# LSH attention with two GLU layers: the hash as four raw fp32 products of 32 columns, codes in rounded fp32

## The chip, the core and the metric

The program runs on one core of a Trainium2 chip. The metric is the device time of one execution in microseconds (us). TensorE (PE) multiplies and transposes, VectorE (DVE), ScalarE (ACT) and GpSimd (POOL) work elementwise, and the SP queue (and ACT's own queue at the start) issues the transfers.

## What is computed

Attention comes first, for 2 batches of 8 heads with 768 tokens and 64 numbers per head. A query sees only the keys whose hash bucket is the same as its own; a bucket is made of the signs of six projections.

```python
q_bits = (np.einsum('bhsd,dk->bhsk', q, proj) > 0).astype(np.int64)
k_bits = (np.einsum('bhsd,dk->bhsk', k, proj) > 0).astype(np.int64)
powers = 2 ** np.arange(n_bits)
q_bucket = np.sum(q_bits * powers, axis=-1)
k_bucket = np.sum(k_bits * powers, axis=-1)
mask = q_bucket[:, :, :, None] == k_bucket[:, :, None, :]
scores = scale * np.matmul(q, k.transpose(0, 1, 3, 2))
scores = np.where(mask, scores, -1000000000.0)
...
return np.matmul(attn, v).astype(np.float32)
```

The softmax of the masked scores is multiplied with v. Two gated layers (512 to 1536 to 512, and 512 to 2048 to 512) follow on all 1536 tokens. The change touches only the hash.

## The kernel before

Attention works on 8 pairs of heads, one after the other. The two heads of a pair share a tile: 64 partitions each (`E` and `O`), 768 tokens along the free dimension. For each pair a `Prep` object makes ready what the next pair needs while the pair before it is in the main loop:

- `UW`, or `scale`, `top` and `rest`: the loaded tile `nat` (named `n` in the profile) is split into `U`, its value rounded to fp32r, and `W`, what is left. For the first pair ACT and DVE do this, for the others POOL.
- `z`: the projections. The table `pz` holds the projection matrix (again as a rounded part and a rest). Twelve products of 384 columns add into one PSUM tile: for queries and keys, `U` with the first part of `pz`, `U` with the rest, and `W` with the first part, each for two halves of the tokens. The table is shifted in its columns so that each of the four cases lands on its own rows of the 72 that a product writes.
- `bits`: ACT takes the sign and writes `bt` in bf16.
- `xp`: four products (`code` times `bt`, 384 columns each, bf16) count for each of the 64 buckets how many bits agree. `Hot` turns that into a one-hot row, big for queries and minus one for keys, which is added to the scores as extra rows of the contraction. DMAs (`copy`, `first_moves`, `swap`) and copies put the pieces of `U`, `W` and the one-hot rows on their partitions.

The scores of a unit (`QK`, 128 queries of one head) are four products of 384 columns; DVE takes the maximum, ACT the exponential (`P`). `Flip` transposes P on TensorE into `pt`, and ACT and DVE write it as two fp16 parts. `pv` multiplies with v in 64 columns of the array per head, so its products come in pairs, one for each half of the columns.

The order on each engine is written out by hand: every step has a time in a table (`AT` for the first and the last pair, `AM` for the six between them, in units of a score tile), and the program is emitted in order of these times. Nothing is reordered by a scheduler. The four parts of `z` stand there as `"Z"`, the sign as `"BITS"`, the code products as `"XP"`.

The first pair's preparation is written out by itself at the start. `warm` runs products of the zeroed tile `bt` while the first loads are under way. In that stretch ACT makes `U`, then copies `H` (line 430) and `B` (line 434) for queries, takes the sign (line 401), copies the second `B`, and writes the one-hot rows `N` and `H` (line 412). The first scores (`sc`, line 474) need `N`.

Of the kernel before, what the change touches and what calls it, by code (L numbers as in the profile page):

```python
# [29 lines left out]
def lsh_attention_glu_act(ctx, tc, qt, kt, v, proj, w_gate, w_val, w_out1, w_in2, w_out2, ident_d, code_d, out):  # L30
    nc = tc.nc
# [22 lines left out]
    proj_sb = const.tile([128, NB], F32, name="proj_sb")  # L54
    ZR = 32 + 4 * NB
    ZW = 72
    Z0 = 32 + 2 * NB
    code_f = const.tile([ZR, 2, 2, 128], F32, name="code_f")
# [3 lines left out]
    pz = const.tile([128, 2, Z0 + ZW], F32R, name="pz")  # L62

    def constants():
        nc.scalar.dma_start(proj_sb, proj)
        nc.scalar.dma_start(code_f, code_d)
        nc.scalar.dma_start(ident, ident_d)
        nc.vector.memset(bt, 0.0)
        nc.vector.memset(pz.bitcast(F32), 0.0)
        nc.gpsimd.memset(code, 0.0)  # L70
        for i, c in enumerate((-TINY, -2.0 * BIG, -float(NB), 0.5, -1.0)):
            nc.vector.memset(cst[:, i:i + 1], c)
        for e, r in ((0, E), (1, O)):
            cs = slice(Z0 + e * NB, Z0 + (e + 1) * NB)
            nc.vector.tensor_copy(pz[r, 0, cs], proj_sb[r])
            nc.vector.tensor_tensor(out=pz[r, 1, cs], in0=proj_sb[r], in1=pz[r, 0, cs].bitcast(F32), op=ALU.subtract)
# [252 lines left out]
    def qbank(k, g):  # L329
# [6 lines left out]
        if next(turn) < 4:  # L336
            nc.tensor.matmul(t, lhsT=code[:, 0, 0, :], rhs=bt, start=True, stop=True, skip_group_check=True)
        return t

    with ExitStack() as actx:  # L340
# [18 lines left out]
        class Prep:  # L359
# [225 lines left out]
        with tc.manual_schedule():  # L585
# [39 lines left out]
            def scale_in():  # L625

                nc.tensor.matmul(idle[:, 2, 0:1], lhsT=code_f[0:1, 0, 0, :], rhs=VS[seq[0]][0][:, 132:133], start=True, stop=True)
# [779 lines left out]
```

## Time and profile before

| what | us |
|---|---|
| median of 3 runs (lowest, highest) | 783.62 (782.73, 785.25) |
| the profiled execution | 782.68 |
| span of the profiled execution, first to last instruction | 780.9 |
| PE busy | 767.5 (98%) |
| DVE busy | 624.8 (80%) |
| ACT busy | 523.5 (67%) |
| POOL busy | 165.3 (21%) |

Attention takes the first 236 us or so, the two gated layers the rest. A share of busy time is a mean over both. The end of a matmul is modelled in the trace: a row's duration holds the time in the pipeline too, so what a product costs in a stream is read from the start of one row to the start of the next.

### The profile page before, as it was taken

To read this page: it belongs to the slowest core of one execution; us is meant where nothing else is said; L and a number is where in the kernel's file an instruction comes from. 1 tells how busy PE (TensorE), PEld (TensorE's weight loads), DVE (VectorE), ACT (ScalarE), POOL (GpSimd) and SP (SyncE) were. 2 spreads that over 40 slices of the span, in tenths; PEclk is the share of its full clock that TensorE was granted. 3 is DMA by queue.
4 is the path that set the end of the run, shared out by engine and by line. 5 is a ranking of instruction groups with operands and counts; after the bars stand their busy time and mean duration, and the time that the engine had idled before them with its cause. 6 is when DMAs were issued, how large, how long until landed. Compare 5 with 4: busy or idle time off the path is not lost.

```text
span 780.9 us, 13062 instructions
## 1 busy us (share of the span) xinstructions
PE 767.5 (98%) x4912; PEld 701.8 (90%) x4912; DVE 624.8 (80%) x1095; ACT 523.5 (67%) x1027; POOL 165.3 (21%) x166
## 2 busy tenths in 40 slices
PE   8999999999999999999999999999999999999997
PEld 5778888888778999999999999998999998898986
DVE  6879999988978978877869869868989867666643
ACT  6988899988975566566555544446666667676653
POOL 5746677864594000000000000000000000000000
PEclk9999999999999999999999999999999999999999
DMA  8845466435101122131122422433332201000002
GB/s 241 201 118 152 92 176 173 130 85 123 32 1 55 55 97 67 55 101 62 55 81 81 136 81 91 126 109 108 108 95 95 81 1 74 8 1 1 0 1 82
DMA packets 41462, 66.98 MB, mean 86 GB/s; under 512 B 5630, under 2 KB 28542, under 8 KB 41398
## 3 DMA queue, kind: packets, MB, share of 16 engines
q1 hardware_dynamic: 40608, 65.30, 28.7%
q8 instruction: 39, 0.64, 0.3%
q10 hardware_dynamic: 790, 0.84, 0.3%
q14 instruction: 25, 0.20, 0.1%
HBM read 45.27 MB, written 3.15 MB: 62 GB/s over the span
## 4 chain that ended last, share of the span: by engine, by line
PE 66%; DVE 1%; ACT 0%; issue 0%; ACTq 0%
PE qa L297 3%; PE qa L296 3%; PE qa L298 3%; PE p L298 3%; PE p L296 3%; PE p L297 3%; PE qb L296 2%; PE y L297 2%; PE y L298 2%; PE y L296 2%; PE qe L296 2%; PE qe L297 2%; PE qe L298 2%; PE qb L297 2%; PE qb L298 2%; PE qa L1167 2%
## 5 line engine op out<-in xcount | busy, mean ns | idle before, releaser
L521 DVE SCALAR_TENSOR_TENSOR PT<-pt,PT 128x512 f16<-128x512 f32 x144 | 95.2, 685 | 13.4 <-ACT PT L518 10.5
L482 DVE TENSOR_REDUCE st<-sc 128x1 f32<-128x768 f32 x96 | 90.5, 948 | 6.6 <-PE sc L474 6.4
L518 ACT ACTIVATE PT<-pt 128x512 f16<-128x512 f32 x144 | 80.6, 596 | 20.9 <-PE pt L509 19.4
L486 ACT ACTIVATE P<-sc,st 128x768 f32<-128x768 f32 x96 | 86.9, 905 | 8.2 <-DVE st L482 8.0
L509 PE MATMUL pt<-ident,P 128*128 128x128 f32 x576 | 78.5, 276 | 2.4 <-DVE PT L521 1.3
L509 PEld LDWEIGHTS pt<-ident,P 128*128 128x128 f32 x576 | 65.0, 141 | 12.9 <-DVE PT L521 7.3
L566 PE MATMUL O<-PT,vh 128*64 128x256 f16 x576 | 53.8, 277 | 0.0
L298 PE MATMUL p<-yh,whl_i 128*128 128x384 f32 x128 | 42.9, 336 | 0.0
L296 PE MATMUL p<-yh,whl_i 128*128 128x384 f32 x128 | 42.9, 335 | 0.0
L297 PE MATMUL p<-yl,whl_i 128*128 128x384 f32 x128 | 42.9, 335 | 0.0
L566 PEld LDWEIGHTS <-vh 128*64 128x64 f16 x576 | 31.3, 109 | 10.5 <-issue 9.8
L1144 ACT ACTIVATE t<-p,cst 128x384 f32<-128x384 f32 x32 | 18.3, 573 | 27.1 <-PE p L298 27.1
L566 PE MATMUL O<-PT,vl 128*64 128x256 f16 x288 | 33.8, 273 | 0.0
L474 PE MATMUL sc<-H,H 128*128 128x384 f32 x96 | 28.3, 376 | 1.1 <-ACT P L486 1.0
L1149 DVE SCALAR_TENSOR_TENSOR gg<-p,t 128x384 f32<-128x384 f32 x32 | 17.7, 554 | 13.3 <-ACT t L1146 13.2
L474 PE MATMUL sc<-N,N 128*128 128x384 f32 x96 | 28.0, 372 | 0.4 <-ACT N L412 0.3
L261 ACT ACTIVATE qb<-qa 128x384 f32<-128x384 f32 x24 | 11.4, 475 | 24.0 <-PE qa L298 13.5
L261 ACT ACTIVATE qd<-qb 128x384 f32<-128x384 f32 x24 | 11.4, 475 | 23.8 <-PE qb L298 20.4
L389 POOL TENSOR_TENSOR W<-n,U 128x768 fp32r<-128x768 f32 x14 | 25.6, 1830 | 0.2
L474 PE MATMUL sc<-U,U 128*128 128x384 f32 x96 | 24.7, 338 | 0.0
L296 PEld LDWEIGHTS p<-yh,whl_i 128*128 128x128 f32 x128 | 24.0, 188 | 0.5
L297 PEld LDWEIGHTS p<-yl,whl_i 128*128 128x128 f32 x128 | 24.0, 188 | 0.5
(1220 smaller groups left out, 2535.2 us busy)
## 6 DMA issues: line engine op xcount, KB each, us to landing
wr_o<-in_moe_w_out_dram SPq DMA_DIRECT2D x28, 512.0 KB, 3.3
H<-U SPq DMA_DIRECT2D x29, 192.0 KB, 3.7
wr_i<-in_moe_w_in_dram SPq DMA_DIRECT2D x8, 512.0 KB, 3.7
wr_i<-in_moe_w_in_dram SPq DMA_DIRECT2D x16, 256.0 KB, 2.8
n<-in_qt_dram SPq DMA_DIRECT2D x8, 384.0 KB, 6.7
n<-in_kt_dram SPq DMA_DIRECT2D x8, 384.0 KB, 6.0
U<-W SPq DMA_DIRECT2D x16, 192.0 KB, 4.9
vr<-in_v_dram SPq DMA_DIRECT2D x8, 384.0 KB, 5.4
```

The lines of the kernel that those rows point to most:

```text
L261: nc.scalar.activation(out=self.new("bcd"[m]), in_=src, func=AF.Copy)
L296: nc.tensor.matmul(ps, lhsT=wh, rhs=rh, start=first, stop=False, **kw)
L297: nc.tensor.matmul(ps, lhsT=wh, rhs=rl, start=False, stop=False, **kw)
L298: nc.tensor.matmul(ps, lhsT=wl, rhs=rh, start=False, stop=last, **kw)
L389: nc.gpsimd.tensor_tensor(out=self.t4[j][1], in0=self.nat[j], in1=f(self.t4[j][0]), op=ALU.subtract)
L474: nc.tensor.matmul(self.sc[:, n, 0:HN], lhsT=M[:, ts], rhs=K[:, n * HN:(n + 1) * HN], start=s0, stop=not s0)
L482: nc.vector.tensor_reduce(out=self.st[:, 0, self.c:self.c + 1], in_=self.sc[:, :, 0:HN], op=ALU.max, axis=AX.XY, negate=True)
L486: nc.scalar.activation(out=self.P, in_=self.sc[:, :, 0:HN], func=AF.Exp, bias=self.st[:, 0, self.c:self.c + 1], scale=1.0, accum_out=self. ...
L509: nc.tensor.transpose(self.ps[m][:, j, :], un[2 * self.n + e].P[:, a, c:c + 128], ident)
L518: nc.scalar.activation(out=self.part(0, m), in_=self.ps[m], func=AF.Copy, scale=PSCALE)
L521: nc.vector.scalar_tensor_tensor(out=self.part(1, m), in0=self.ps[m], scalar=PSCALE, in1=self.part(0, m), op0=ALU.mult, op1=ALU.subtract)
L566: nc.tensor.matmul(O_ps[r, 0:GN], lhsT=vv[m][:, e, i * D:(i + 1) * D], rhs=PT[:, l, e * NI + i, :], start=(s == 0), stop=(s == len(steps) ...
```

## The change

The projections become four products of the raw loaded tile with the raw projection matrix, both in plain fp32, one for each of queries and keys and token half. Each writes 32 rows of its own in PSUM, that is, uses 32 columns of the array. All four are issued at one place of the program, where the last part of `z` stood; the three earlier places in the tables are gone. `bt` and `code` become fp32r, on all 128 partitions: each of the four cases has its 32 partitions, and a code product contracts over these 32 rows instead of 128. The tables are loaded straight into place (`pz` by two transfers behind a memset), so the casts on DVE go; `code` is smaller. At the start the sign of the first pair stands ahead of the copies on ACT, `swap` ahead of the copies too, and `warm` has 16 products of fp32r instead of 18 of bf16.

```diff
-    code = const.tile([128, 2, 2, 128], BF16, name="code")
-    bt = const.tile([128, HN], BF16, name="bt")
+    ZC = 32
+    pz = const.tile([128, ZC], F32, name="pz")
+    ones = const.tile([1, 128], F32, name="ones")
+    code_f = const.tile([128, 128], F32, name="code_f")
+    code = const.tile([128, 128], F32R, name="code")
+    bt = const.tile([128, HN], F32R, name="bt")
...
-        nc.scalar.dma_start(proj_sb, proj)
+        nc.gpsimd.memset(pz, 0.0)
+        for e, r in ((0, E), (1, O)):
+            nc.scalar.dma_start(pz[r, e * NB:(e + 1) * NB], proj[r])
...
-            def z(self, lo, hi):
-                if lo == 0:
-                    self.z_ps = pA.tile([128, 512], F32, tag="mm", bufs=MMB, name=f"z_{self.b}_{self.p}")
-                steps = [(j, c, t, n) for j in range(2) for c, t in ((0, 0), (1, 0), (0, 1)) for n in range(2)]
-                for m in range(lo, hi):
-                    j, c, t, n = steps[m]
-                    s = Z0 - 32 * n - 2 * NB * j
-                    nc.tensor.matmul(self.z_ps[0:ZW, 0:HN], lhsT=pz[:, c, s:s + ZW], rhs=self.t4[j][t][:, n * HN:(n + 1) * HN], start=(m == 0), stop=(m == len(steps) - 1))
+            def z(self):
+
+                self.z_ps = pA.tile([128, 512], F32, tag="mm", bufs=MMB, name=f"z_{self.b}_{self.p}")
+                for g in range(4):
+                    j, n = divmod(g, 2)
+                    nc.tensor.matmul(self.z_ps[ZC * g:ZC * g + ZC, 0:HN], lhsT=pz, rhs=self.nat[j][:, n * HN:(n + 1) * HN], start=True, stop=True, skip_group_check=True)
 
             def bits(self):
-                nc.scalar.activation(out=bt[0:ZR], in_=self.z_ps[0:ZR, 0:HN], func=AF.Sign, bias=cst[0:ZR, 0:1])
+                nc.scalar.activation(out=bt, in_=self.z_ps[:, 0:HN], func=AF.Sign, bias=cst[:, 0:1])
+
+            def codes(self, ps, j, n):
+
+                r = slice(ZC * (2 * j + n), ZC * (2 * j + n) + ZC)
+                nc.tensor.matmul(ps, lhsT=code[r], rhs=bt[r], start=True, stop=True)
...
-            warm(18)
+            warm(16)
             pp, p1 = Prep(*seq[0]), Prep(*seq[1])
+            nc.vector.tensor_copy(code, code_f)
             pp.UW(0)
             pp.first_moves(0)
             pp.UW(1)
             pp.first_moves(1)
-            nc.vector.tensor_copy(code[0:ZR], code_f)
+            pp.z()
+            pp.bits()
             pp.first_copy(nc.gpsimd.tensor_copy, 0)
...
-            pp.first_copy(nc.scalar.copy, 1)
-            pp.rest_copy(0)
-            pp.z(0, 12)
             for j in range(2):
                 pp.swap(j)
-            pp.bits()
+            pp.rest_copy(0)
             pp.rest_copy(1)
+            pp.first_copy(nc.scalar.copy, 1)
...
-                "Z": (-1.4412, 0.5823, 0.8230, 1.7397),
+                "Z": (1.7397,),
```

On PE the place where the second pair of heads runs and the third is made ready shows what moves. Before, its twelve products stand in four groups of three, of which the last three groups are among these rows (`sc` are scores, `pt` transposes of P, `r` transposes of the row sums, `z` the projections):

```order
L398 MATMUL z_2_532<-U_0_2_446,pz 72x384
L398 MATMUL z_2_532<-W_0_2_447,pz 72x384 x2
L509 MATMUL pt_2_617<-ident,P_0_1_5_462 128x128 x4
L509 MATMUL pt_0_626<-ident,P_1_0_0_555 128x128 x4
L398 MATMUL z_2_532<-U_0_2_450,pz 72x384 x3
L474 MATMUL sc_1_1_1_642<-N_0_1_137,N_0_1_133 128x384 x2
L474 MATMUL sc_1_1_1_642<-W_0_1_135,W_0_1_131 128x384 x2
L398 MATMUL z_2_532<-U_0_2_450,pz 72x384
L398 MATMUL z_2_532<-W_0_2_451,pz 72x384 x2
L743 MATMUL r_0_1_5_657<-ident,rb_0_1_5_655 128x128 x2
```

Only the four new products are left, in two rows between the scores and the transposes of the row sums, where the last group was:

```order
L507 MATMUL pt_2_588<-ident,P_0_1_5_440 128x128 x4
L507 MATMUL pt_0_597<-ident,P_1_0_0_529 128x128 x4
L472 MATMUL sc_1_1_1_610<-N_0_1_132,N_0_1_128 128x384 x2
L472 MATMUL sc_1_1_1_610<-W_0_1_130,W_0_1_126 128x384 x2
L391 MATMUL z_2_615<-n_0_2_217,pz 32x384 x2
L391 MATMUL z_2_615<-n_0_2_219,pz 32x384 x2
L740 MATMUL r_0_1_5_627<-ident,rb_0_1_5_625 128x128 x2
```

The first group of three (ahead of the rows shown) is gone as well, and everything else on PE keeps its order. In this place ACT's order does not change.

At the start ACT's order does change. Before, it makes `U` for queries and keys, two copies, the sign `bt`, one more copy, and then the one-hot rows from `xq`:

```order
L379 ACTIVATE U_0_0_126<-n_0_0_78 128x768
L430 CAST H_0_0_124<-U_0_0_122 64x768
L434 CAST B_140<-W_0_0_123 64x768
L401 ACTIVATE bt<-z_0_158,cst 56x384
L434 CAST B_144<-W_0_0_127 64x768
L412 ACTIVATE N_0_0_125<-xq,cst 64x768
L412 ACTIVATE H_0_0_124<-xq,cst 64x768
```

Now the sign comes right behind `U`, and all three copies stand between it and the one-hot rows:

```order
L374 ACTIVATE U_0_0_121<-n_0_0_78 128x768
L394 ACTIVATE bt<-z_0_144,cst 128x384
L432 CAST B_136<-W_0_0_118 64x768
L432 CAST B_140<-W_0_0_122 64x768
L428 CAST H_0_0_119<-U_0_0_117 64x768
L410 ACTIVATE N_0_0_120<-xq,cst 64x768
L410 ACTIVATE H_0_0_119<-xq,cst 64x768
```

Two copies have moved from ahead of the sign to behind it. On DVE the cast of `code` moves ahead of the two `W`, and the four small instructions that made `pz` are gone.

## Rows read from the trace of the kernel before

**Rows 1.** The page: busy time and share, and TensorE's granted clock in 40 slices.

```profile
PE 767.5 (98%) x4912; PEld 701.8 (90%) x4912; DVE 624.8 (80%) x1095; ACT 523.5 (67%) x1027; POOL 165.3 (21%) x166
PEclk9999999999999999999999999999999999999999
```

**Rows 2.** Windows: stretch, then busy us and instructions by engine, clock, DMA.

```profile
0.00:12.00 12.00, 9.90 (x44) 5.74 (x45) 6.66 (x21) 7.53 (x9) 6.72 (x9) 1.00 0.77 232
12.00:40.00 28.00, 26.22 (x195) 21.37 (x194) 23.93 (x37) 22.63 (x49) 17.05 (x18) 1.00 0.85 213
96.00:124.00 28.00, 28.00 (x256) 24.49 (x254) 26.02 (x43) 25.18 (x53) 22.08 (x24) 1.00 0.64 173
```

**Rows 3.** Waits from 12 to 236 us: us in total, times, longest.

```profile
PE pt L509 <- DVE PT L521: 1.3, 3, 0.9
...
PEld L566 <- issue: 9.3, 44, 0.3
...
PEld L407 <- issue: 3.5, 18, 0.2
```

**Rows 4.** Instructions of line 398: duration ns (min/median/max), first and last start.

```profile
L398 PE MATMUL z<-U,pz x64: 331/337/469, 5.7 to 183.1; 128*72 128x384 f32 x64
L398 PE MATMUL z<-W,pz x32: 331/338/398, 6.8 to 183.4; 128*72 128x384 f32 x32
```

**Rows 5.** Timeline of PE around the last group of z: start, us, instruction.

```profile
100.82 0.51 PE L474 MATMUL sc<-W,W 128*128 128x384 f32 x2
101.17 0.34 PE L398 MATMUL z<-U,pz 128*72 128x384 f32 x1
101.34 0.51 PE L398 MATMUL z<-W,pz 128*72 128x384 f32 x2
101.69 0.38 PE L743 MATMUL r<-ident,rb 128*128 128x128 f32 x2
```

**Rows 6.** Instructions of line 627, the one raw fp32 product: duration, starts.

```profile
L627 PEld LDWEIGHTS idle<-vrow,code_f x2: 181/182/184, 19.2 to 19.3; 1*128 1x128 f32 x2
L627 PE MATMUL idle<-vrow,code_f x2: 245/256/266, 19.2 to 19.3; 1*128 1x1 f32 x2
```

**Rows 7.** Timeline of PE from 106.02 us.

```profile
106.02 1.04 PE L509 MATMUL pt<-ident,P 128*128 128x128 f32 x8
106.81 0.60 PE L474 MATMUL sc<-N,N 128*128 128x384 f32 x2
...
109.82 0.28 PE L566 MATMUL O<-PT,vl 128*64 128x256 f16 x2
110.03 0.34 PE L407 MATMUL xp<-bt,code 128*128 128x384 bf16 x1
110.30 0.30 PE L566 MATMUL O<-PT,vh 128*64 128x256 f16 x2
110.43 0.28 PE L566 MATMUL O<-PT,vl 128*64 128x256 f16 x2
110.54 0.28 PE L566 MATMUL O<-PT,vh 128*64 128x256 f16 x2
```

**Rows 8.** Timeline of the first 11 us, all engines.

```profile
1.11 4.92 PE L619 MATMUL idle<-bt 128*128 128x384 bf16 x18 [1.11 <-DVE bt L68]
...
5.49 0.85 ACT L379 ACTIVATE U<-n 128x768 fp32r<-128x768 f32 x1 [0.54 <-DMA n<-in_kt_dram]
5.74 0.99 PE L398 MATMUL z<-U,pz 128*72 128x384 f32 x4
...
8.42 0.58 ACT L401 ACTIVATE bt<-z,cst 56x384 bf16<-56x384 f32 x1 [0.50 <-PE z L398]
...
8.90 0.82 ACT L434 CAST B<-W 64x768 fp32r<-64x768 f32 x1
...
9.62 0.90 ACT L412 ACTIVATE N<-xq,cst 64x768 fp32r<-64x768 f32 x1
...
10.62 0.63 PE L474 MATMUL sc<-N,N 128*128 128x384 f32 x2 [0.27 <-ACT N L412]
```

More of the change, by code (lines that the diff above doesn't have):

```diff
@@ L53, in lsh_attention_glu_act @@
     ident = const.tile([128, 128], F32, name="ident")
[L54 to L58, printed above, removed]
-    code = const.tile([128, 2, 2, 128], BF16, name="code")
-    bt = const.tile([128, HN], BF16, name="bt")
+    ZC = 32
[4 more added lines that the diff above has]
+    bt = const.tile([128, HN], F32R, name="bt")
     cst = const.tile([128, 5], F32, name="cst")
-    pz = const.tile([128, 2, Z0 + ZW], F32R, name="pz")
     def constants():
-        nc.scalar.dma_start(proj_sb, proj)
+        nc.gpsimd.memset(pz, 0.0)
+        for e, r in ((0, E), (1, O)):
+            nc.scalar.dma_start(pz[r, e * NB:(e + 1) * NB], proj[r])
         nc.scalar.dma_start(code_f, code_d)
         nc.scalar.dma_start(ident, ident_d)
-        nc.vector.memset(bt, 0.0)
-        nc.vector.memset(pz.bitcast(F32), 0.0)
-        nc.gpsimd.memset(code, 0.0)
+        nc.vector.memset(bt.bitcast(F32), 0.0)
+        nc.vector.memset(ones, 1.0)
         for i, c in enumerate((-TINY, -2.0 * BIG, -float(NB), 0.5, -1.0)):
             nc.vector.memset(cst[:, i:i + 1], c)
[L73 to L76, printed above, removed]
     def f(ap):
@@ L336, in qbank @@
         if next(turn) < 4:
-            nc.tensor.matmul(t, lhsT=code[:, 0, 0, :], rhs=bt, start=True, stop=True, skip_group_check=True)
+            nc.tensor.matmul(t, lhsT=code, rhs=bt, start=True, stop=True, skip_group_check=True)
         return t
@@ L406, in xp @@
                     if n is None or n == a:
-                        nc.tensor.matmul(self.x_ps[:, a] if n is None else self.x_ps, lhsT=code[:, a, j, :], rhs=bt, start=True, stop=True)
+                        self.codes(self.x_ps[:, a] if n is None else self.x_ps, j, a)
             def Hot(self, j, dst, r, n=None):
@@ L625, in scale_in @@
             def scale_in():
-                nc.tensor.matmul(idle[:, 2, 0:1], lhsT=code_f[0:1, 0, 0, :], rhs=VS[seq[0]][0][:, 132:133], start=True, stop=True)
+                nc.tensor.matmul(idle[:, 2, 0:1], lhsT=ones, rhs=VS[seq[0]][0][:, 132:133], start=True, stop=True)
             def scale_keep():
@@ L645, in lsh_attention_glu_act @@
                 p1.rest(j)
-            nc.gpsimd.memset(code_f[0:1, 0, 0], 1.0)
-            pp.first_copy(nc.scalar.copy, 1)
-            pp.rest_copy(0)
-            pp.z(0, 12)
             for j in range(2):
                 pp.swap(j)
-            pp.bits()
+            pp.rest_copy(0)
             pp.rest_copy(1)
+            pp.first_copy(nc.scalar.copy, 1)
             xq = sc_tile("xq")
@@ L657, in lsh_attention_glu_act @@
                 for a in range(2):
-                    nc.tensor.matmul(xk[a] if j else xq[:, a, 0:HN], lhsT=code[:, a, j, :], rhs=bt, start=True, stop=True)
+                    pp.codes(xk[a] if j else xq[:, a, 0:HN], j, a)
             for dst, r in ((3, E), (2, O)):
@@ L825, in lsh_attention_glu_act @@
                         for m in range(1, 3):
-                            at(T["Z"][3] + 0.01 * m + 0.001 * j, 0, q, on, q + 1, "copy", j, m)
+                            at(T["Z"][0] + 0.01 * m + 0.001 * j, 0, q, on, q + 1, "copy", j, m)
                         at(T["H"][2 * j + 1] + 0.03, 0, q, on, q + 1, "copy", j, 3)
                         at(T["H"][3] + 0.035 + 0.005 * j, 0, q, on, q + 1, "copy", j, 4)
-                        at(T["TOP"][j] + 0.002 if q else T["Z"][3] + 0.03, 0, q, on, q + 1, "copy", j, 5)
-                    at(max(T["H"][3], T["Z"][3]) + 0.06, 0, q, on, q + 1, "done")
+                        at(T["TOP"][j] + 0.002 if q else T["Z"][0] + 0.03, 0, q, on, q + 1, "copy", j, 5)
+                    at(max(T["H"][3], T["Z"][0]) + 0.06, 0, q, on, q + 1, "done")
                 if q + 2 < NQ:
@@ L1374, in _tables @@
     sgn = (2 * bit - 1).astype(np.float32)
-    code = np.zeros((32 + 4 * nb, 2, 2, 2 * nbk), np.float32)
+    code = np.zeros((128, 2 * nbk), np.float32)
     for n in range(2):
@@ L1378, in _tables @@
             for e in range(2):
-                r = 32 * n + nb * (2 * j + (e ^ j))
-                code[r:r + nb, n, j, (1 - e) * nbk:(2 - e) * nbk] = sgn.T
+                r = 32 * (2 * j + n) + nb * (e ^ j)
+                code[r:r + nb, (1 - e) * nbk:(2 - e) * nbk] = sgn.T
     return {"ident": np.eye(128, dtype=np.float32), "code": code}
```

2 lines of the change are left out of this document (1 added, 1 removed), and 2 rows, old and new, of the table AT.

## The prediction, on record before the run

> **What bounds the kernel now.** The page comes first: PE is busy for 98% of the span, and its clock stands at its upper level, 2.4 GHz, in all 40 slices [rows 1]. That share is a mean, so the stages come next, as windows. From 96 to 124 us, which is attention in full swing, PE is busy 28.00 of 28 us, while DVE has about 2 us to spare and ACT nearly 3 [rows 2]. From 12 to 40 us, the first pair of heads, PE lacks 1.8 us and from 0 to 12 us 2.1 us [rows 2]: there a chain of single steps sets the pace. The waits agree: over the whole of attention PE's longest wait in total is 1.3 us, for DVE's second halves of P [rows 3], which is next to nothing. So a microsecond more or less of PE's stream between 40 and 236 us is a microsecond of the result, and at the start the chain through ACT has to be followed. The two layers behind 236 us are untouched.
>
> **What is removed from PE.** The projections are 64 + 32 products [rows 4], twelve for each of eight pairs. A row's duration (0.33 us) holds the pipeline, so the price is read between starts: one product from 101.17 to 101.34 us, two more to 101.69 [rows 5], 0.17 us each. That is 384 columns at one column per cycle. Twelve are 2.04 us per pair, and they fit between scores and transposes without a gap (scores at 100.82, two products, then 101.17).
>
> **What a raw fp32 product costs.** The trace has one, and of a single column: it stands as two weight loads and two matmuls [rows 6], so one instruction is two passes. How long 384 columns take in a pass it doesn't show. The nearest rows are the transposes of P, raw fp32 too: eight of 128 columns go by from 106.02 to 106.81 us [rows 7], 0.10 us each, or 0.11 by their own length (1.04 less the last one's 0.27, over seven). That is nearly two cycles a column; three of them make 384 columns, 0.30 to 0.33 us. I take 0.32 us for a pass, 0.64 for a product. The lower bound is the fp32r rate, 0.17 for a pass. The Trainium skill (FP8 and Floating Point Precision, TensorE Precision Notes) says that true fp32 makes four passes through the array; by it a product would be 4 x 0.16 = 0.64 us, an estimate, and the sum the same.
>
> **Whether the four overlap.** Each writes its own 32 columns of the array. The trace has products side by side in half the columns each: the pairs with v start at 110.43 and 110.54 us [rows 7], 0.11 us for two products of 256 columns, the time of one. So different columns do work at once. But PE starts matmuls in order, and the second pass of a product needs the columns of its first. With passes 1a 1b 2a 2b 3a 3b 4a 4b, 1b waits for 1a; 2a starts with 1b, 2b waits for 2a, and 3a starts with 2b. This makes five steps, 5 x 0.32 = 1.6 us per pair. If nothing overlaps it is 8 x 0.32 = 2.56 us, if all four run at once 2 x 0.32 = 0.64. I take the staircase: it needs only what the pairs show.
>
> **What is added by changing the cut of the array.** Between PV's pairs and a product over all columns there is a loss. The last pair starts at 109.82 us and should take 0.11, but the code product starts at 110.03: 0.10 lost. It takes 0.16, but the next pair starts at 110.30: 0.11 lost [rows 7]. The weight loads show it as a wait called "issue", 44 times before PV and 18 times before the code product, 0.2 us each [rows 3]: the load isn't made ahead as elsewhere. The Trainium skill (TensorEngine Tiling (Array Packing), Key Properties) says that a change of tiling mode drains TensorE; it speaks against this change, and the trace agrees with 0.1 us each way. I put 0.11 us on each new change. The block of projections in 32 columns has two (scores before, transposes behind). The code products contract over 32 rows now, a cut that the trace doesn't show; bounds are nothing and 0.11 us, and I take 0.11, as PV's columns are the only cut seen. In the six middle pairs three of the four code products gain one change each (the order has them between PV and something over the whole array; the fourth stands in PV on both sides and pays already). Together five changes, 0.55 us. In the first pair the four stand between transposes and scores: eight, with the block ten, 1.1 us.
>
> The code products themselves stay at 0.17 us: 384 columns, fp32r as fast as bf16 [rows 5, 7]. The sign's time hangs on 384 numbers per partition, which stay. Casts and memsets that go from DVE and POOL lie in the first microseconds, beside the loads.
>
> **The sum in the stream.** Six middle pairs: 1.6 - 2.04 + 0.55 = +0.11 us each, together +0.7. The pair prepared in the first pair's loop: 1.6 - 2.04 + 1.1 = +0.66; PE has some idle there, I count half, +0.3.
>
> One long block in place of four short ones could starve DVE and ACT. Ahead of the block stand two transposes' groups and a unit of scores: DVE has two halves of P and a maximum to do, ACT two more and an exponential, some 2 us, as long as the block. The sign isn't later than before either, since the groups left out earlier bring everything forward. I count nothing; without that cover it is what the block exceeds 2 us by, which is the serial rival.
>
> **The start.** Before, warm-up products run from 1.11 us to the first projection at 5.74; the sign runs from 8.42, half a microsecond after ACT was free, since it waited for the last of them, one copy follows at 8.90, and the one-hot `N` at 9.62, which releases the first scores at 10.62 [rows 8]. Now two late warm-up products are fewer (0.16 each), but a bigger memset of `bt` comes first, so the projections begin at about 5.55; the keys are there at 5.49 [rows 8]. They end 1.6 us later, with 0.17 for the pipeline at 7.3, and the sign begins at 7.35. ACT gives 0.48 us to the sign (8.42 to 8.90) and 0.72 to a copy (8.90 to 9.62) [rows 8]; three copies stand ahead of `N` now, so `N` begins at 7.35 + 0.48 + 3 x 0.72 = 10.0 in place of 9.62: the saved time is eaten by two copies that had been done while ACT waited for z. +0.4 us. What is late next is the first maximum and exponential; nothing else is awaited there, so I count it in full.
>
> **The sum**: +0.7 + 0.3 + 0.4 = +1.4 us. The profiled execution took 782.68 us (780.9 of span and 1.8 around it), which becomes 784.1; the median of the runs lies 0.9 above it, so I say **785.0 us**. A measurement of this kernel can tell about 0.3% from no change, 2.4 us: this is no change.
>
> **The rivals.**
> - *Nothing overlaps*: the second pass's weight load in the same columns holds up what is behind it, and passes run one by one. For it: two loads to a product [rows 6], and that no raw product in a part of the columns is in the trace; against it: the pairs with v. Middle pairs 2.56 - 2.04 + 0.55 = +1.07 each, +6.4; first loop half of +1.62; the start 0.96 later, +1.36: **+8.6 us, 792**. It decides from about 1.9 us a block on.
> - *All four at once*: 0.64 us a block. Middle pairs -0.85 each, -5.1; first loop -0.15; the start -0.5: **-5.8 us, 778**. Against it is the second pass behind the first in order. The Trainium skill (TensorE: Matmul & The Clock Gate, Part 3) says so: products in different columns start about 4 ns apart, and a pack lasts as long as one.
> - *A pass at the fp32r rate*, 0.17 us: the staircase is 0.85 us, middle pairs -0.64 each, -3.8; first loop nothing; the start -0.35: **-4.1 us, 779.5**. The transposes speak against it, unless weight loads and not columns set their pace.
> - *The code products pay nothing* for 32 rows: -0.33 x 6 and -0.4, so **-1 us, 782.6**, still no change.
>
> **Chances.** The staircase 0.52 (with or without the code products' price: same 0.37, slower 0.10, faster 0.05), nothing overlaps 0.30 (slower), all at once 0.10 and the fast pass 0.04 (faster), and 0.04 for something at the start that makes it slower (a late table, a clock that falls in the longer gap before the first scores). Faster 0.19, same 0.37, slower 0.44. The range leaves out the parallel case and the far end of the serial one: **779.5 to 793**; the likeliest case alone is 782.5 to 787.5.
>
> **What would show it.** In the profile after: projections as 8 matmuls a pair; the time from the first one's start to the transposes behind it, 1.8 us by the staircase, 2.8 serial, 0.9 parallel, and whether the starts of passes come 0.32 us apart in twos; "issue" waits of the weight loads at every code product; `N` at about 10.0 us at the start; the end of attention 1 to 2 us later. I am wrong if PE turns out to wait for ACT or DVE behind the block, or if a pass isn't 0.32 us.

## The result, and the profile after

The changed kernel takes 789.16 us (median of 6 runs, 787.24 to 790.68) against 783.17 us before (median of 6): a ratio of 1.0072, 95% interval 1.0059 to 1.0084. It is slower by 6 us. The profiled execution took 789.67 us with a span of 787.9 us, 7.0 us more than before's span.

The page of the changed kernel, busy time and PE's granted clock, to set beside [rows 1]:

```profile
PE 770.1 (98%) x4878; PEld 697.0 (88%) x4878; DVE 622.8 (79%) x1091; ACT 524.2 (67%) x1027; POOL 164.0 (21%) x165
PEclk8999999999999999999999999999999999999999
```

PE has 34 matmuls fewer, is busy 2.6 us longer, and no longer holds its clock in the first slice. Where the 7 us arise is read from the starts of the sign (one ACT instruction for each pair): the time from one to the next is the period of a pair. In us:

| kernel | first sign | to the 2nd | first loop | 2nd to 6th loop | last sign | span |
|---|---|---|---|---|---|---|
| before | 8.4 | 13.1 | 25.3 | 27.1, 28.0, 27.3, 27.3, 27.3 | 183.8 | 780.9 |
| after | 7.7 | 16.5 | 27.2 | 27.1, 28.0, 28.0, 28.0, 28.0 | 190.3 | 787.9 |

So the second sign is 2.6 us late, the first loop adds 1.85 us, the last three of these loops (the steady pairs) 0.7 us each, and 0.5 us arises behind the last sign. The first three parts have their rows below.

**The steady pair.** PE's timeline of the changed kernel around one block of projections (start, us, instruction), beside [rows 5]:

```profile
155.44 1.09 PE L507 MATMUL pt<-ident,P 128*128 128x128 f32 x8
...
157.46 1.26 PE L507 MATMUL pt<-ident,P 128*128 128x128 f32 x8
...
159.52 1.26 PE L507 MATMUL pt<-ident,P 128*128 128x128 f32 x8
...
161.40 0.85 PE L391 MATMUL z<-n,pz 128*32 128x384 f32 x8
162.19 0.44 PE L740 MATMUL r<-ident,rb 128*128 128x128 f32 x2
```

The block is eight matmuls, and the next instruction starts 0.79 us behind its first. Its own instructions, in a view that groups them by start (first line up to 161.45 us):

```profile
L391 PE MATMUL z<-n,pz x4: 510/510/510, 161.4 to 161.4; 128*32 128x384 f32 x4
...
L391 PE MATMUL z<-n,pz x8: 486/498/510, 161.4 to 161.8; 128*32 128x384 f32 x8
```

Four start together at 161.4 us, the other four up to 161.8. The experiment with one column group below shows that passes in the same columns run one behind the other, so these are all four first passes at once, then all four second passes.

Between the transposes `pt` the reader is to see their distance: 2.02 and 2.06 us. The same place of the kernel before, with three projections in each of these gaps:

```profile
149.34 1.03 PE L509 MATMUL pt<-ident,P 128*128 128x128 f32 x8
...
151.43 1.17 PE L509 MATMUL pt<-ident,P 128*128 128x128 f32 x8
...
153.67 1.04 PE L509 MATMUL pt<-ident,P 128*128 128x128 f32 x8
```

There it was 2.09 and 2.24 us. Taking 0.5 us of products out of a gap has brought 0.07 to 0.18 us. DVE's rows of the changed kernel show why:

```profile
156.71 1.29 DVE L519 SCALAR_TENSOR_TENSOR PT<-pt,PT 128x512 f16<-128x512 f32 x2
157.92 0.95 DVE L480 TENSOR_REDUCE st<-sc 128x1 f32<-128x768 f32 x1
158.78 1.29 DVE L519 SCALAR_TENSOR_TENSOR PT<-pt,PT 128x512 f16<-128x512 f32 x2
```

Two halves of P and one maximum follow each other without a pause, every 2.07 us. From 154.4 to 162.4 us DVE is busy 7.91 of 8 us (ACT 7.45); in the 20 us ahead of that, which hold the pair's four code products, only 16.9 of 20. The waits from 12 to 236 us (PE, then its weight loads) say what holds the transposes now, beside [rows 3]:

```profile
PE pt L507 <- DVE PT L519: 2.6, 2, 2.3
...
PEld pt L507 <- DVE PT L519: 10.3, 30, 2.6
PEld L564 <- issue: 8.7, 42, 0.3
...
PEld xp L399 <- issue: 3.6, 19, 0.2
```

The view of before that [rows 3] is taken from has this line for the loads as well:

```profile
PEld pt L509 <- DVE PT L521: 7.3, 23, 1.3
```

A transpose's buffer is free only when DVE has written the second half of P out of it; the transposes' loads wait 10.3 us for that, before 7.3. In the windows of [rows 2] PE had nothing to spare. It still seems so (27.88 of 28.00 us busy from 134.4 to 162.4 us), because such a wait sits inside a group of eight: the row grows from 1.03 to 1.26 us and counts as busy.

**The start.** All engines of the changed kernel, beside [rows 8]:

```profile
1.30 5.49 PE L617 MATMUL idle<-bt 128*128 128x384 f32 x16 [1.30 <-DVE bt L68]
...
6.72 0.85 PE L391 MATMUL z<-n,pz 128*32 128x384 f32 x8
7.66 0.58 ACT L394 ACTIVATE bt<-z,cst 128x384 fp32r<-128x384 f32 x1 [1.46 <-PE z L391]
...
8.18 0.82 DVE L634 CAST code<-code_f 128x128 fp32r<-128x128 f32 x1 [6.75 <-DMA code_f<-in_code_dram]
8.92 1.81 DVE L375 SCALAR_TENSOR_TENSOR W<-n,U 128x768 fp32r<-128x768 f32 x2
...
9.90 1.70 ACT L432 CAST B<-W 64x768 fp32r<-64x768 f32 x2 [1.66 <-DVE W L375]
...
12.24 0.89 ACT L410 ACTIVATE N<-xq,cst 64x768 fp32r<-64x768 f32 x1
...
13.23 0.98 PE L472 MATMUL sc<-N,N 128*128 128x384 f32 x2 [2.83 <-ACT N L410]
```

The sign comes 0.8 us earlier than before. But `code` is cast ahead of the two `W` on DVE now, and its table lands at 8.2 us; `W` starts at 8.92 where it started at 5.33, the copies `B` wait for `W`, and the one-hot `N` stands behind them. The first scores start at 13.23 in place of 10.62 us. PE has little to do from 10 to 13 us, and its clock falls. Windows, in the columns of [rows 2]:

```profile
10.00:11.00 1.00, 0.41 (x2) 0.00 (x0) 1.00 (x2) 0.96 (x2) 0.93 (x2) 0.54 0.42 117
12.00:13.00 1.00, 0.00 (x0) 0.00 (x0) 0.73 (x2) 1.00 (x2) 1.00 (x1) 0.50 0.88 194
15.00:16.00 1.00, 1.00 (x5) 1.00 (x4) 0.85 (x1) 0.12 (x1) 0.97 (x1) 0.50 1.06 375
```

A granted clock of 0.50 is the lower level, 1.2 GHz: there two score products take 0.64 us where they take 0.35 at 2.4 GHz.

**The first loop.** The SP queue, DVE and PE of the changed kernel:

```profile
37.10 2.70 SPq L450 DMA_DIRECT2D H<-U  x4
39.84 0.83 SPq L529 DMA_DIRECT2D vrow<-vm  x1
...
44.76 0.28 DVE L538 TENSOR_REDUCE vrow<-vrow 1x1 f32<-1x129 f32 x1 [2.78 <-DMA vrow<-vm]
...
46.90 1.65 PE L507 MATMUL pt<-ident,P 128*128 128x128 f32 x8 [2.25 <-DVE PT L519]
```

DVE stands 2.78 us in a step that belongs to v (the maximum of the next pair's v, which a small transfer brings to one partition), and PE waits 2.25 us for DVE. Before, these were 2.02 and 0.92 us:

```profile
41.45 0.27 DVE L540 TENSOR_REDUCE vrow<-vrow 1x1 f32<-1x129 f32 x1 [2.02 <-DMA vrow<-vm]
...
43.60 1.26 PE L509 MATMUL pt<-ident,P 128*128 128x128 f32 x8 [0.92 <-DVE PT L521]
```

Here too the clock follows:

```profile
44.00:46.00 2.00, 0.65 (x4) 0.33 (x2) 1.18 (x4) 0.00 (x0) 0.00 (x0) 1.00 0.00 0
46.00:48.00 2.00, 1.10 (x7) 0.92 (x8) 2.00 (x5) 1.40 (x3) 0.34 (x1) 0.90 0.32 43
48.00:50.00 2.00, 2.00 (x11) 1.53 (x13) 1.69 (x4) 1.54 (x4) 0.28 (x2) 0.50 1.07 394
```

### The profile page after: what moved, and what is told of

It reads as the page before. It is cut to its first block, busy times and chain, and to the rows that moved or that the text cites. A ratio compares the mean times of both kernels' runs of the same rounds, so it can differ in the third digit from the quotient of the medians.

```text
span 787.9 us, 13001 instructions
## 1 busy us (share of the span) xinstructions
PE 770.1 (98%) x4878; PEld 697.0 (88%) x4878; DVE 622.8 (79%) x1091; ACT 524.2 (67%) x1027; POOL 164.0 (21%) x165
## 4 chain that ended last, share of the span: by engine, by line
PE 65%; DVE 1%; ACT 0%; issue 0%
PE qa L291 3%; PE qa L292 3%; PE qa L293 3%; PE p L293 3%; PE p L291 3%; PE p L292 3%; PE y L292 2%; PE y L293 2%; PE y L291 2%; PE qe L291 2%; PE qb L291 2%; PE qe L292 2%; PE qe L293 2%; PE qb L293 2%; PE qb L292 2%; PE qa L1164 2%
## 5 line engine op out<-in xcount | busy, mean ns | idle before, releaser
L516 ACT ACTIVATE PT<-pt 128x512 f16<-128x512 f32 x144 | 81.4, 598 | 22.8 <-PE pt L507 21.6
L507 PE MATMUL pt<-ident,P 128*128 128x128 f32 x576 | 80.3, 278 | 4.2 <-DVE PT L519 2.8
L1141 ACT ACTIVATE t<-p,cst 128x384 f32<-128x384 f32 x32 | 18.4, 574 | 27.2 <-PE p L293 27.2
L472 PE MATMUL sc<-N,N 128*128 128x384 f32 x96 | 30.0, 394 | 3.4 <-ACT N L410 2.8
L256 ACT ACTIVATE qb<-qa 128x384 f32<-128x384 f32 x24 | 11.4, 475 | 24.1 <-PE qa L293 13.5
L256 ACT ACTIVATE qd<-qb 128x384 f32<-128x384 f32 x24 | 11.4, 475 | 23.8 <-PE qb L293 20.4
```

The source lines that it names most:

```text
L256: nc.scalar.activation(out=self.new("bcd"[m]), in_=src, func=AF.Copy)
L472: nc.tensor.matmul(self.sc[:, n, 0:HN], lhsT=M[:, ts], rhs=K[:, n * HN:(n + 1) * HN], start=s0, stop=not s0)
L507: nc.tensor.transpose(self.ps[m][:, j, :], un[2 * self.n + e].P[:, a, c:c + 128], ident)
L516: nc.scalar.activation(out=self.part(0, m), in_=self.ps[m], func=AF.Copy, scale=PSCALE)
```

## The experiments

The theory that they test: the block of projections is cheap (0.79 us), but what it replaces had cost next to nothing where it stood; the pair is longer by the code products over 32 rows; the rest is lost at the start and in the first loop, by waits. Its rivals: PE's stream is the bound and the block costs more than its rows show; or the start alone makes the difference. All times below are from sign to sign, in the order of the table above.

### What the block is worth: all four in one column group

```diff
-nc.tensor.matmul(self.z_ps[ZC * g:ZC * g + ZC, 0:HN], lhsT=pz, ...
+nc.tensor.matmul(self.z_ps[0:ZC, 0:HN], lhsT=pz, ...
```

The sign then runs on these 32 rows only. Of the four products only the last is kept and the other bits stay at zero, so this kernel leaves the hash out; the run is read for its time alone.

> The changed kernel with all four projection products in the same 32 columns (only the last one's rows are kept, and the sign and the codes of the other three are left at zero, so the hash is not computed). Theory A (the four products run at once because they stand in different columns; a pass takes 0.32 us): the block from its first start to the next transposes goes from 0.79 to about 2.7 us, steady period +1.9 us at most. Rival (a pass takes 0.16 us and the four would be short in any columns): block about 1.4 us.

A single run: 801.88 us, span 800.1. Loops 27.9, 28.9, 29.9, 29.9, 29.9, 29.9 from the first on. PE's timeline:

```profile
139.87 2.77 PE L391 MATMUL z<-n,pz 128*32 128x384 f32 x8
142.56 0.44 PE L740 MATMUL r<-ident,rb 128*128 128x128 f32 x2
```

Eight passes in the same columns take 2.69 us, 0.34 each, one behind the other. So a pass costs what the prediction had taken from the transposes (0.32), and it is the four column groups that make 0.79 us of it. The steady pair grows by 1.9 us (28.0 to 29.9) for 1.9 us of block: what is added here is paid in full. Whether products taken away come back in full is tested by the run with a third of them, below.

### What the code products over 32 rows cost: alone in the kernel before, and undone in the kernel after

In the kernel before, with its bf16 tables:

```diff
-lhsT=code[:, a, j, :], rhs=bt
+lhsT=code[32 * a:32 * a + 32, a, j, :], rhs=bt[32 * a:32 * a + 32]
```

> The kernel before with one edit: in the loops its bf16 code products contract over the 32 rows that hold their bits, not over all 128; the start's four are left. Theory A (a change of the array's cut is what costs, whatever the type): steady period from 27.3 to about 27.7 us, first loop +0.8, total +3 to +3.5 us, about +0.4%. Rival (it is the fp32r weight load of 181 ns in place of 96 that isn't hidden): within 1 us of the kernel before.

785.41 us (784.74 to 787.39, 6 runs), ratio 1.0033 (1.0019 to 1.0046); span 783.5. Loops 26.2, 27.2, 27.9, 27.7, 27.7, 27.7: the first loop +0.9, the steady pairs +0.4. The products themselves last as long as before (332 ns, their loads 90 ns). So the smaller cut costs 2.6 us of span by itself, without any change in the projections. Of the first loop's 0.9, how much the cut costs directly isn't shown: DVE's wait for `vrow<-vm` has grown there too, from 2.02 to 2.77 us.

In the kernel after, back over 128 rows, with a table for each of the four cases:

```diff
-nc.tensor.matmul(ps, lhsT=code[r], rhs=bt[r], start=True, stop=True)
+nc.tensor.matmul(ps, lhsT=code[:, 2 * j + n], rhs=bt, start=True, stop=True)
```

> The changed kernel with code products that contract over all 128 rows again (four tables in fp32r, zero outside their 32 rows); projections, types and the start's order as changed. Theory A (the cut to 32 rows and its weight loads cost about 0.6 us in each steady pair and 0.8 in the first loop, which is why the shorter projections give nothing): the steady period falls from 28.0 to about 27.4 us, total 3.5 to 4.5 us less than the changed kernel, about +0.2%. Rival B (the block of projections in one place starves DVE and ACT, the code products' cut is harmless): the period stays at 27.9 to 28.0 us and the total within 1 us of the changed kernel.

789.63 us (789.45 to 789.96), ratio 1.0083 (1.0068 to 1.0098). The pair does what the theory says: loops 25.8, 26.9, 27.7, 27.4, 27.5, 27.5, so 0.5 us of each steady pair come back. The time does not: the second sign is at 27.8 us, 3.6 us later than in the kernel after, since the table takes four casts on DVE ahead of `W`. Its `W`, from the timeline of the start:

```profile
9.54 4.07 DVE L376 SCALAR_TENSOR_TENSOR W<-n,U 128x768 fp32r<-128x768 f32 x2
```

The two `W` take 4.07 us where they took 1.81. They now run beside POOL's `U` and `W` of the next pair; that this is the cause isn't shown. The first scores start at 16.1 us.

The fp32r table adds something else, which the weight loads of the code products show from 60 to 236 us, in the kernel after (durations in ns):

```profile
L399 PEld LDWEIGHTS xp<-bt,code x21: 181/181/182, 62.8 to 203.4; 32*128 32x128 f32 x21
```

The same of the kernel before:

```profile
L407 PEld LDWEIGHTS <-code x20: 95/96/98, 75.4 to 196.2; 128*128 128x128 bf16 x20
```

The weight load takes 181 ns in place of 96, and a code product isn't loaded ahead (the "issue" waits), so it stands in the stream. A code product between PV's pairs in the kernel after, to set beside [rows 7]:

```profile
143.07 0.43 PE L399 MATMUL xp<-bt,code 32*128 32x384 f32 x1
143.44 0.30 PE L564 MATMUL O<-PT,vh 128*64 128x256 f16 x2
```

The next pair of PV starts 0.37 us behind it, in [rows 7] 0.27 us; bf16 codes over 32 rows have 0.26 in this place. That is 0.1 us for the type, four times a pair. Added up over the four code products of a steady pair, from the start of the instruction ahead to the start of the one behind, the stream holds 1.59 us before, 1.87 with bf16 over 32 rows and 2.29 after: 0.7 us more, of which the cut is 0.3 and the type 0.4. The steady loops agree with it: 27.1 to 27.3 us with bf16 codes over 128 rows and the new projections (below), 27.4 to 27.5 with fp32r over 128 rows, 28.0 with fp32r over 32 rows. So the code products make the steady pair's 0.7. The 0.5 us behind the last sign goes with them too: from the last sign to the end it is 597.1 us before and 597.6 after, and 597.1 to 597.3 in the three kernels that have the new projections and codes over 128 rows.

The Trainium skill (TensorE: Matmul & The Clock Gate, Weight-path perf modes) says that the fast weight load is on for 128 weights of an input that is not FP32. The trace agrees if fp32r counts as FP32: its load takes 181 ns, as raw fp32's does in [rows 6], and bf16's 90 to 98.

### What the projections were worth: a third of them in the kernel before

Only the four products of `U` with the first part of `pz` are left, one in each of the old places; the products with the rests are left out:

```diff
-for c, t in ((0, 0), (1, 0), (0, 1)) for n in range(2)]
+for c, t in ((0, 0),) for n in range(2)]
...
-at("Z", i, q, on, q + 1, "z", 3 * i, 3 * i + 3)
+at("Z", i, q, on, q + 1, "z", i, i + 1)
```

> The kernel before with only 4 of its 12 projection products per pair (the rounded values with the rounded table; the rest parts are left out, so that a sign very near zero can differ), one at each of the four places. Theory A (where the projections stand, PE waits for DVE or stands ready anyway, so a shorter projection is worth only a part of itself): of 8 x 0.17 = 1.36 us per steady pair at most 0.8 comes back, period 26.5 us or more. Rival (PE's stream is the bound, as the prediction had it): period 27.3 - 1.36 = 25.9 us, total -9 us.

782.57 us (10 runs, before 783.22), ratio 0.9994 (0.9979 to 1.0009): no difference that can be told. Eight products fewer are 1.36 us of PE's stream, and the steady loops are 27.2, 27.1, 27.2 in place of 27.3. In the total a loss hides a gain: the second sign is 0.9 us earlier, but the first loop is 1.4 us longer (26.7), as DVE waits 3.27 us for `vrow<-vm` there (2.02 before) and the granted clock is 0.50 from 44.2 to 47.7 us behind it. PE's timeline shows why the steady pairs stay as they are:

```profile
149.36 1.03 PE L509 MATMUL pt<-ident,P 128*128 128x128 f32 x8
...
151.37 1.26 PE L509 MATMUL pt<-ident,P 128*128 128x128 f32 x8
...
153.44 1.26 PE L509 MATMUL pt<-ident,P 128*128 128x128 f32 x8
```

The transposes are 2.01 and 2.07 us apart, as in the kernel after. In this stretch DVE's two halves of P and its maximum, 2.07 us, set the pace, and the twelve products had stood in gaps of it. The rival that PE's stream is the bound falls.

### The new projections alone, and in another place

The kernel after with the old code products (bf16, 128 rows; the table comes as bf16 and needs no cast) and with before's order on ACT at the start, and `ident` loaded by SP's queue in place of ACT's:

```diff
-code = const.tile([128, 128], F32R, name="code")
+code = const.tile([128, 4, 128], BF16, name="code")
...
-nc.tensor.matmul(ps, lhsT=code[r], rhs=bt[r], start=True, stop=True)
+nc.tensor.matmul(ps, lhsT=code[:, 2 * j + n], rhs=bt, start=True, stop=True)
...
 pp.z()
-pp.bits()
+warm(8)
```

> The four raw products without what came with them: codes in bf16 over all 128 rows again (their table comes from DRAM in that form, so that no cast is needed), the start in the order of the kernel before, with eight warm-up products behind the projections. Theory A (the code products and the start made the loss; the shorter projections are worth next to nothing where they stand): steady period 27.2 to 27.3 us, first scores at 10 to 10.6 us with the clock up, total within 1.5 us of the kernel before. Rival B (the projections' block itself costs something): period 27.6 us or more.

785.17 us (10 runs), ratio 1.0016 (1.0003 to 1.0029); span 784.4. Loops 27.8, 26.8, 27.8, 27.3, 27.2, 27.1: the steady pair is as before or up to 0.2 us shorter. So the block costs nothing there, and what four products in place of twelve save on PE (about 1 us a pair) is not there either. The start and the total missed what was expected. By the third sign (51.0 us, before 46.9) the kernel has lost 4.1 us. At the start the scores begin at 12.39 us, behind a transfer that lands at 12.25 (the larger table landed at 10.2), and the clock is 0.50 from 12.2 to 15.7 us:

```profile
12.39 0.98 PE L470 MATMUL sc<-N,N 128*128 128x384 f32 x2 [0.85 <-DMA N<-U]
```

In the first loop DVE waits 4.16 us for `vrow<-vm`.

Then the same with the block moved one gap earlier, ahead of the transposes:

```diff
-                "Z": (1.7397,),
+                "Z": (0.5823,),
```

> As e8, with the four products of the middle pairs one unit earlier, between two units' scores and transposes where PE waits for DVE in the changed kernel. Theory A: they cost nothing there, the period falls by 0.3 to 0.6 us against e8, total 2 to 4 us less than the kernel before. Rival (the place doesn't matter, since what PE gains in one place DVE takes in the next): within 0.1 us per pair of e8.

786.68 us (10 runs), ratio 1.0042 (1.0027 to 1.0057), loops 28.4, 27.6, 27.6, 27.6 from the third on, with the copies that follow the block kept in their place: 0.3 to 0.6 us a pair worse. The theory had expected a gain here, and that part of it falls. PE's waits from 60 to 236 us, and DVE behind one block:

```profile
PE r L740 <- DVE PT L517: 2.1, 6, 0.4
```

```profile
159.54 1.29 DVE L517 SCALAR_TENSOR_TENSOR PT<-pt,PT 128x512 f16<-128x512 f32 x2 [0.51 <-ACT PT L514]
```

The block delays the transposes behind it, these delay DVE, and DVE is what the stretch waits for. This gap had held 0.5 us of projections for next to nothing (2.24 us between the transposes before, 0.17 over DVE's 2.07); it doesn't hold 0.8: the transposes around the block start 2.66 us apart.

### The start: the cast behind `W`, and the old order on ACT

```diff
-            nc.vector.tensor_copy(code, code_f)
             pp.UW(0)
...
             pp.first_moves(1)
+            nc.vector.tensor_copy(code, code_f)
             pp.z()
```

> The changed kernel with one line moved: on DVE the cast of the code table stands behind the two W of the first pair, as it did before the change, and no longer ahead of them. Theory A (the start is lost because DVE waits for the table's load, to 8.18 us in the changed kernel, with both W and so ACT's copies behind it): first scores at about 11 us in place of 13.23, the clock no longer falls at 10 us, and the kernel gains 2 to 2.5 us on the changed one, to about +0.4% over the kernel before. Rival (the start is lost by the order on ACT, sign ahead of three copies): first scores at 12.5 us or later, less than 1 us gained.

788.39 us (4 runs), ratio 1.0071 (1.005 to 1.0092). The first scores start at 11.47 in place of 13.23 us, and the second sign comes 1.2 us earlier, at 22.9. The span of the profiled execution is 1.0 us shorter, not as much as expected; the median, 0.8 us less, can't be told from the changed kernel's. `N` is ready at 11.27, but the scores wait for a transfer that lands at 11.34, at a clock that has fallen all the same:

```profile
11.47 0.98 PE L472 MATMUL sc<-N,N 128*128 128x384 f32 x2 [1.01 <-DMA N<-U]
```

With ACT's order of before on top (the sign behind two copies), and the late cast kept:

> As e1, and ACT's order at the start is that of the kernel before as well (one copy of U and one of W ahead of the sign, one behind). Theory A: ACT's order is worth 0.5 to 1 us more than e1, first scores at about 10.0 to 10.5 us, total about +0.3% over before; the steady pairs stay at 28.0 us each. Rival (ACT's order carries the start): 2 us or more gained over e1.

788.65 us, ratio 1.007 (1.0055 to 1.0086), first scores at 11.47 too, second sign at 23.0 (22.9 in the run above). ACT's order does move `N`: it begins at 9.58 in place of 10.38 us. But the transfer `N<-U` lands at 11.33 in this run too, so the 0.8 us stay hidden behind it. The order on ACT, which the prediction had costed at the start, is worth nothing here; without that late transfer it might be worth up to 0.8 us, which no run shows.

### The first loop, and the clock

In the run with the late cast the maximum of v is ready at 34.6 us, but SP issues its transfer behind four others, at 39.2. One number of the table puts the maximum (on DVE, from 33.6 to 30.2 us) and its transfer ahead of them; all else is as in the run with the late cast:

```diff
-                "VR": (9.39,),
+                "VR": (8.78,),
```

> The kernel with the late cast (e1) with one more number changed: VR, the place of the maximum over v in the first pair's table, from 9.39 to 8.78, so that the DMA vrow<-vm is issued ahead of the four H<-U (2.73 us of SP's time) in place of behind them. Theory A: the first loop is 1.7 us longer than before's because DVE waits for that DMA (3.02 us at line 538), PE runs empty behind it and its clock falls. Then the wait is gone, PE's clock stays at 2.4 GHz from 40 to 52 us, the first loop (sign to sign) takes 25.0 to 25.8 us in place of 27.2, and the run takes about 787.0. Theory B: in the first loop DVE and ACT are behind PE anyway and the wait only sits where the slack is; then PE waits elsewhere, the loop stays at 26.7 or more, and the time at 788.2 to 788.5.

785.34 us (12 runs, before 783.52), ratio 1.0019 (1.001 to 1.0028); span 782.3. Rows of its SP and DVE:

```profile
31.16 0.55 SPq L529 DMA_DIRECT2D vrow<-vm  x1
...
39.86 0.26 DVE L538 TENSOR_REDUCE vrow<-vrow 1x1 f32<-1x129 f32 x1
```

DVE's wait is gone, the clock stays at 1.00 from 40 to 54 us, and the first loop takes 23.9 us: 3.2 us less than with the late cast alone, more than expected, and 1.4 less than in the kernel before, which has such a wait itself. The wait and the clock behind it were the whole loss there.

This run shows the clock's price at the start as well, since up to the first loop its order is that of the run with the late cast. Windows of that run:

```profile
10.00:11.00 1.00, 0.47 (x2) 0.00 (x0) 0.97 (x3) 1.00 (x2) 0.85 (x2) 0.50 0.44 114
12.00:13.00 1.00, 1.00 (x5) 1.00 (x4) 0.00 (x0) 0.19 (x1) 1.00 (x2) 0.50 0.83 181
```

And this one:

```profile
10.00:11.00 1.00, 0.04 (x1) 0.00 (x0) 0.97 (x3) 1.00 (x2) 0.88 (x2) 1.00 0.41 126
12.00:13.00 1.00, 1.00 (x6) 0.74 (x6) 0.62 (x1) 0.23 (x1) 1.00 (x2) 1.00 0.99 230
```

Up to there the program is the same, and it is granted 0.50 in one execution and 1.00 in the other. The first scores start at 11.5 and 11.4 us, the second sign comes at 22.9 and at 21.6 us. By these two executions the lower clock costs 1.3 us at the start. With the clock up, scores that start 0.8 us later than before (11.40, before 10.62) cost next to nothing by the second sign (21.6, before 21.5). Over the 12 runs, those with a mean clock of 0.994 to 0.996 have spans of 783.7 to 784.6 us, those with 0.998 or 0.999 have 782.2 to 783.1.

The same number changed in the kernel before:

> The kernel before with VR from 9.39 to 8.78 alone. Theory A: the 2.02 us that DVE waits there for vrow<-vm, with the 0.92 us of PE behind it, go; the first loop takes 24.4 to 24.9 us in place of 25.4, and the run 782.3 to 782.8 in place of 783.2 (ratio 0.999). Theory B: PE catches up in the first loop in any case, no difference (ratio 1.000).

782.07 us (12 runs, before 783.52), ratio 0.9981 (0.9972 to 0.999); first loop 24.6 us in place of 25.3, all others as they were. It is the fastest of all kernels here, and it holds nothing of the change. With the wait gone on both sides and the cast late, the two profiled executions, both at the upper clock, tell what is left of the change: 2.1 us of span (782.3 against 780.2). The first loop is 0.6 us shorter (23.9 against 24.6), the three steady loops together 2.1 us longer, and 0.7 us arises behind the last sign.

Two runs were to keep the clock up at the start by more products. The first read a tile that wasn't complete:

```diff
+            for i in range(16):
+                nc.tensor.matmul(idle[:, 0:3], lhsT=code, rhs=pp.t4[0][0][:, 0:HN], start=True, stop=True)
```

> e10 with sixteen more products (code times U, 384 columns, result unused) on PE between the code products of the first pair and its first scores, to keep PE busy while it waits for N and for the DMA N<-U. Theory A: the start is lost to the clock at 1.2 GHz; with the fill the first scores still start at about 11.5, but at 0.35 us a pair in place of 0.64, and the next sign comes at 21.5 to 22.0 in place of 22.9; the time is 1 us below that of e10. Theory B: behind the first scores DVE's maxima and ACT's exponentials set the pace, whatever the clock; then the next sign comes within 0.4 us of where it is in e10.

790.47 us, ratio 1.0088 (1.0075 to 1.0101). It says nothing of either theory: half of that tile's partitions come by the transfer U<-W, and PE stood until 12.15 us for it, with the fill, most of it at the lower clock (16 in 5.20 us), in front of the scores. The second sign came at 27.9 us.

The second read `bt`, which nothing overwrites there:

```diff
+            warm(10)
```

> e10 with ten more warm products of bt behind the code products of the first pair (about 1.7 us at 0.17 us each, between 9.3 us and the first scores at 11.4, which read nothing that a transfer brings). In e10 the granted clock of single runs lies between 0.994 and 0.999 and their spans between 782.2 and 784.6 us. Theory A: at the start PE's idle 2 us let its clock fall to 1.2 GHz in some runs and not in others, and that is worth 1.2 to 1.4 us; with the fill every run shows 0.998 or more, the spans are 782.0 to 783.2, and the median is 784.2 (ratio 1.0006). Theory B: the clock falls in the fill's place anyway or costs nothing in the chain through ACT and DVE; the median stays at 785.3 (ratio 1.002).

784.8 us (12 runs, before 783.13), ratio 1.002 (1.0005 to 1.0035). The clock was 1.00 in every microsecond from 8 to 17 us of the profiled execution, and 10 of 12 runs have 0.998 or more (5 of 12 without the fill). But the median against before is the same as without it, and the spans go from 782.2 to 786.8 us, wider than the theory said. In the profiled execution the code table landed late (its cast starts at 9.18 us, 8.02 without the fill), so the fill ended behind `N` and the scores began at 12.32 in place of 11.40 us. The clock can be kept; what the fill gains it gives back here. That part is inconclusive.

## Why the prediction was right or wrong

The measured 789.16 us lies in the range, and slower had the largest chance. That is luck for the most part: of the 0.44 for slower, 0.30 stood for passes that run one by one, and they ran side by side; the time came from things that the sum has small or not at all. The forecast itself, no change at 785.0 us, did not come: +1.4 us was said, +7.0 us of span were measured. By its steps:

- **What bounds the kernel.** "So a microsecond more or less of PE's stream between 40 and 236 us is a microsecond of the result": wrong downwards. It was read from PE's busy 28.00 of 28 us [rows 2] and from PE's waits of 1.3 us [rows 3]; the line of the same view in which the transposes' weight loads wait 7.3 us for DVE was not used. Where the projections stood, DVE is as full as PE, and PE's rows hide short waits in groups of eight. Removing 1.36 us of products gave 0.1 to 0.2; adding 1.9 us cost 1.9. This is the step that failed for the steady pair: twelve products out and the short block in is about 1 us less on PE (2.04 less 0.79 and two changes of the cut at the prediction's 0.11), and was worth 0 to 0.2.
- **A pass of a raw product**, 0.32 us: right (0.34 in one column group).
- **The staircase**, 1.6 us: wrong. The passes run four at a time, 0.79 us to the next instruction; the prediction had named 0.9 us as the sign of the parallel case. "All four at once", given 0.10, is what happens. The prediction's time for that rival, 778, was wrong all the same, as it valued PE's time in full. The Trainium skill (TensorE: Matmul & The Clock Gate, Part 3) had said that products in different columns run at the same time. The trace agrees: four starts within 0.02 us at 161.4.
- **The code products over 32 rows**: right in mechanism (each now waits at its load: 4 "issue" waits in one steady pair, before 3), too small in size. The cut was costed at 0.33 us a pair; it took 0.3 of PE's stream and 0.4 of the pair. "fp32r as fast as bf16" was wrong by 0.1 us for each product, by its longer weight load. Together 0.7. Unlike the projections, they stand where PE's time counts.
- **The first loop**, +0.3: measured +1.85, but by a wait that is not in the sum: the transfer `vrow<-vm` behind four others on SP, 0.8 us longer for DVE than before, and the clock that PE's longer wait for DVE lost. Without the wait the change gains 0.6 us there.
- **The start**, +0.4: measured +2.6. The sign's time came out within 0.3 us (7.35 said, 7.66) by luck. The projections began at 6.72, not at 5.55, since the sixteen warm-up products took about 0.32 us each to the last one, where 0.16 had been counted for the two left out; and the block, with its results, took 0.94 us, not 1.8. The step that failed is to follow only the chain through ACT and to put the moves on DVE at nothing: the cast of `code` was moved ahead of `W`, where it waits 6.75 us for its table. `N` begins at 12.24, said 10.0; with the cast put back it is 10.38. The copies ahead of `N` cost 0.8 us of `N` between ACT's two orders, but the scores wait for a transfer that lands later still. And the step that counts a late first score in full failed: with the clock up 0.8 us became 0.1. Putting the cast back gives 1.2 us, the clock another 1.3 in the executions in which it holds; the remaining 0.1 us (21.6 against 21.5) is what the start's other edits cost. A late table and a falling clock had been given 0.04 as a rival.

Two things stay open. The transfer `N<-U` lands 4.0 to 6.4 us behind its issue in the kernels with the new tables, 5.0 in the changed one, against 3.3 before. The number of packets on the other queue is not the cause by itself: 358 before and 448 after, but 304 in the kernel with the table in bf16, where it takes 6.4 us. And the second and third loops do not show the 0.7 us (27.1 and 28.0 in both kernels); the runs don't tell what else sets their length.

## What to carry to other kernels

A busy share of 100% doesn't make an engine the bound: look at how far apart its repeated groups start, whether another engine's rows stand end to end at the same distance, and take work out of one gap to see whether that distance shrinks. When work moves on an in-order queue, ask of every step that moved what it waits for, a table's cast and a small transfer too; here these two, with the clock that fell behind them, cost more than all the products together. Before products go to a wider type or a smaller cut of the array, look at their weight loads: a product that can't be loaded ahead pays its load in the stream.

## What the hardware showed that was not expected

Raw fp32 products in four column groups run side by side in both their passes: 0.79 us for four of 384 columns, 2.69 us in one group. Four fp32r products over different groups of 32 rows do the same: at the start of the kernel after, all four begin within 0.01 us (9.14 and 9.15) and the next product starts at 9.52. DVE's two `W` took 1.81 us beside POOL's scaling of `n`, and 4.07 us beside POOL's own `U` and `W` of the next pair; the cause isn't shown. The same order of instructions with nearly the same pause on PE kept its clock in one execution and lost it in another.
